# Two early loads issued by ScalarE instead of SyncE, and unit 3's clip and exponential moved up, in a fused gated-attention and gated-MLP kernel

## The chip, the cores and the metric

The kernel runs on one core of one Trainium2 chip. The metric is the time of one execution in microseconds (us), as the device reports it; the time of before is the median of 3 runs. A profile is one execution taken by the hardware profiler. Engine names are those of its rows: PE (TensorE matmuls), PEld (its weight loads), DVE (VectorE), ACT (ScalarE), POOL (GpSimd), SP (SyncE, which only issues transfers here).

## The reference

```python
def _attn_ref(q, k, v, f_logit):           # B=4, H=8, S=768, D=48
    f = 1.0 / (1.0 + np.exp(-f_logit))
    for t in range(S):
        state = f[:, :, t, :, None] * state + np.einsum('bhd,bhe->bhde', k[:, :, t], v[:, :, t])
        y[:, :, t] = np.einsum('bhd,bhde->bhe', q[:, :, t], state)

def _moe_ref(x, w_in, w_spatial, b_spatial, w_out):   # x: (4, 768, 384), d_ff 1024
    h = np.maximum(x @ w_in, 0.0)
    u, v = (h[..., :d_ff // 2], h[..., d_ff // 2:])
    v_n = (v - mean(v)) / np.sqrt(var(v) + 1e-06)
    v_s = np.einsum('ts,bsd->btd', w_spatial, v_n) + b_spatial[None, :, None]
    return (u * v_s) @ w_out
```

The output of the attention, with its heads joined, is the `x` of the second part.

## The kernel before

The recurrence is worked in 24 **units** n = 0 to 23 of 128 time steps (four batches of six). Inside a unit the decay is turned into running sums of logarithms, keys and queries are scaled by exponentials of these sums, and the unit is then two 64-step chunks of ordinary matmuls plus a carried state. The second part (named V, U, S, P and O in the plan) is dense matmul work on what the units leave.

There is no scheduler. `PLAN` is one long list of steps, written by hand or by a search, and the kernel emits the steps in that order. Each engine runs its own instructions in the order of emission, and waits where data or a buffer is missing. A step named `x:n` calls `step_x(n)`; one step issues on one engine, mostly. `BESIDES` lists steps that run on another engine, or in another variant, than their default.

The steps that matter here, by unit n:

- `LF:n` loads the logits (for the first eight units from `fn`, 192 KB) into `ins[n % 3]`; `LK:n` loads keys and queries (512 KB) into the same tile, `LQ:n` the values (192 KB); `LV:i` loads 768 KB of words of `w_in`. The profile names the tiles `fkq`, `val` and `words`. All are issued by SP.
- `c:n` clips the logits (DVE L371, for units in `BESIDES` POOL), `e:n` is an exponential and a logarithm (ACT L375, L376), `z:n` sums along time by a triangular matmul (PE L386), `g:n` and `h:n` are two exponentials of the sums (ACT L397 and L392).
- `k:n` scales the keys (DVE L403; it needs `LK:n` and `g:n`), `q:n` the queries (DVE L407; it needs `LK:n` and `h:n`).
- `X:n` makes the scores (PE L432; it needs `k:n` and `q:n`), `m:n` masks them (DVE L442), `w:n` copies a part of them (ACT L438), `YS:n` multiplies scores by values (PE L484), `kv:n` makes what the unit adds to the state (PE L456), `r0:n`, `r1:n` add this to the state (DVE L462 to L470), `r2:n` decays it, `Yq:n` multiplies queries by the state (PE L496), `ys:n` copies the result out (ACT L500), `xt:n` transposes it (PE L509).
- `ca:V,i` scales the high words of a weight (ACT L307), `ct:V,i` puts low and high words together (three DVE instructions, L312 to L314; the second needs `ca`).
- `D:1,2,512` is two matmuls with no use for the result.

`ins` has three tiles, so unit 3 reuses unit 0's: `LF:3` can be issued only when `k:0`, the last reader of unit 0's logits, is done on DVE.

Of the kernel before, what the change touches and what calls it, by code (L numbers as in the profile page):

```python
# [1004 lines left out]
```

## Time and profile before

| | |
|---|---|
| time, median of 3 | 338.81 us (338.53 to 338.96) |
| time of the profiled execution | 337.91 us |
| its span, first to last instruction | 336.2 us |
| PE busy | 324.4 us, 96% of the span |
| DVE busy | 252.4 us, 75% |
| ACT busy | 182.7 us, 54% |
| POOL busy | 39.7 us, 12% |
| bytes moved by DMA | 38.37 MB |
| granted TensorE clock, mean | 0.999 |

PE is busy for nearly the whole span, so the time is PE's work plus PE's idle time. The idle time lies almost wholly in the first 25 us, and this is where the change stands. The row of shares over the whole span does not show this; the stretches and the waits do.

### The profile page before, as it was taken

The numbers are of one execution on the slowest core, as the hardware profiler recorded it, in microseconds if no ns is written. First come the engines' busy times: TensorE is split into PE (matmuls) and PEld (weight loads), VectorE is DVE, ScalarE is ACT, GpSimd is POOL, SyncE is SP. The second block draws the span as 40 slices with busy tenths as digits, with TensorE's granted clock in tenths as the row PEclk, the third lists the DMA queues.
The fourth block names the chain that finished last, engine by engine and source line by source line (L and its number), as shares of the span: only waits on it lengthen the run. The fifth ranks groups of instructions, "written<-read, shape, count | busy, mean of one in ns | idle before, by whom it ended". The sixth has DMA issues, their size and how long they took to land.

```text
span 336.2 us, 10500 instructions
## 1 busy us (share of the span) xinstructions
PE 324.4 (96%) x4558; PEld 303.5 (90%) x4558; DVE 252.4 (75%) x498; ACT 182.7 (54%) x389; POOL 39.7 (12%) x44
## 2 busy tenths in 40 slices
...
GB/s 230 368 225 280 268 176 225 218 173 47 152 89 237 41 89 155 82 62 126 137 120 142 96 73 202 156 0 24 2 0 0 49 0 25 71 0 26 48 34 118
DMA packets 16581, 38.37 MB, mean 114 GB/s; under 512 B 1552, under 2 KB 11792, under 8 KB 16528
## 3 DMA queue, kind: packets, MB, share of 16 engines
...
q14 instruction: 15, 0.12, 0.1%
HBM read 32.90 MB, written 4.72 MB: 112 GB/s over the span
## 4 chain that ended last, share of the span: by engine, by line
PE 93%; DMA 3%; DVE 1%; ACT 1%; issue 1%; SPq 0%; DVEq 0%; ACTq 0%
PE mm L664 15%; PE mm L547 13%; PE mm L650 13%; PE mm L803 12%; PE mn L739 8%; PE bp L432 5%; PE mm L739 5%; PE bp L496 4%; PE bp L484 3%; PE mn L803 3%; PE mn L650 3%; PE mm L509 2%; PE bp L456 2%; PE mn L547 2%; DMA fkq<-fkq 2%; DMA fkq<-fn 1%
## 5 line engine op out<-in xcount | busy, mean ns | idle before, releaser
L371 POOL TENSOR_SCALAR fkq<-fkq 112x512 f32<-112x512 f32 (+1 forms) x13 | 22.5, 1729 | 140.2 <-DMA fkq<-fkq 121.8
L789 DVE TENSOR_TENSOR gl<-uT,gh 128x384 fp32r<-128x384 f32 x29 | 16.6, 580 | 19.9 <-ACT gh L785 19.6
L785 ACT CAST gh<-uT 128x384 fp32r<-128x384 f32 x29 | 14.4, 511 | 20.0 <-DVE uT L781 9.8
L392 ACT ACTIVATE F<-fkq 112x512 f32<-112x512 f32 x16 | 10.1, 632 | 26.6 <-DVE fkq L381 14.9
L432 PE MATMUL bp<-q,fkq 48*64 48x112 f32 x768 | 23.6, 260 | 0.1
L403 DVE SCALAR_TENSOR_TENSOR fkq<-fkq 112x512 f32<-112x512 f32 x24 | 16.7, 694 | 5.9 <-ACT fkq L397 4.7
L432 PEld LDWEIGHTS bp<-q,fkq 48*64 48x64 f32 x768 | 19.0, 133 | 2.1 <-issue 1.4
L664 PE MATMUL mm<-w_sph,vnh 128*128 128x384 f32 x96 | 20.1, 345 | 0.0
L381 DVE TENSOR_TENSOR_SCAN fkq<-runs,fkq 112x512 f32<-112x512 bf16 x16 | 19.4, 1217 | 0.5 <-ACT fkq L376 0.4
L664 PE MATMUL mm<-w_spl,vnh 128*128 128x384 f32 x96 | 19.5, 338 | 0.0
L664 PE MATMUL mm<-w_sph,vnl 128*128 128x384 f32 x96 | 19.5, 338 | 0.0
L547 PE MATMUL mm<-w_inh,xTh 128*128 128x512 f32 x63 | 19.2, 412 | 0.0
L650 PE MATMUL mm<-xTh,w_inh 128*128 128x384 f32 x78 | 18.7, 348 | 0.0
L442 DVE TENSOR_TENSOR sc<-bp,mask 128x512 f32<-128x512 f32 x24 | 16.4, 684 | 2.5 <-ACT W L438 2.1
L407 DVE TENSOR_TENSOR q<-fkq,F 112x512 f32<-112x512 f32 x24 | 16.7, 694 | 2.1 <-ACT F L392 2.0
L547 PE MATMUL mm<-w_inl,xTh 128*128 128x512 f32 x63 | 18.1, 396 | 0.0
L547 PE MATMUL mm<-w_inh,xTl 128*128 128x512 f32 x63 | 18.0, 394 | 0.0
L650 PE MATMUL mm<-xTl,w_inh 128*128 128x384 f32 x78 | 17.9, 338 | 0.0
L650 PE MATMUL mm<-xTh,w_inl 128*128 128x384 f32 x78 | 17.9, 337 | 0.0
L484 PEld LDWEIGHTS bp<-val,sc 64*64 64x64 f32 x768 | 13.9, 134 | 4.3 <-issue 1.5
L484 PE MATMUL bp<-val,sc 64*64 64x48 f32 x768 | 16.1, 220 | 1.4 <-DVE sc L442 0.9
L664 PEld LDWEIGHTS mm<-w_spl,vnh 128*128 128x128 f32 x96 | 17.1, 188 | 0.0
...
## 6 DMA issues: line engine op xcount, KB each, us to landing
...
val<-vv SPq DMA_DIRECT2D x24, 192.0 KB, 4.5
out<-osb SPq DMA_DIRECT2D x24, 192.0 KB, 2.4
fkq<-fkq SPq DMA_DIRECT2D x8, 512.0 KB, 5.5
...
fkq<-fn SPq DMA_DIRECT2D x8, 192.0 KB, 4.1
...
```

The costliest lines, as they stand in the source:

```text
L371: (nc.gpsimd if beside("c", n) else nc.vector).tensor_scalar(f, f, -LOGIT_MOST, None, op0=ALU.max)
L381: return nc.vector.tensor_tensor_scan(f[0:DP], runs, f[0:DP], 0.0, op0=ALU.mult, op1=ALU.add)
L403: nc.vector.scalar_tensor_tensor(k, f, 1.0 / F_LEAST, k, op0=ALU.min, op1=ALU.mult)
L407: nc.vector.tensor_tensor(q_of(n)[:, :, :, 0:C], *(x.rearrange("p (j c t) -> p j c t", c=T // C, t=C) for x in (parts(n)[2], Fs[n % 2])), ...
L432: nc.tensor.matmul(sc[to, e, cs], k[dr, at:at + C], q_of(n)[dr, j, chunk], start=True, stop=True)
L484: nc.tensor.matmul(y[to, e, cs], s[rows, keys[e]], v[rows, hd], start=j == 0, stop=False, skip_group_check=True)
L547: nc.tensor.matmul(acc, xs[:, c, ut * P:(ut + 1) * P], ws[:, c, G:FF], start=i == 0, stop=i == 3 * KX - 1)
L650: nc.tensor.matmul(acc[:, 0:TH], ws[:, kx, cs], xs[:, kx, :], start=i == 0, stop=i == 3 * KX - 1)
L664: nc.tensor.matmul(acc[:, 0:TH], vns.of((b, ks))[va][:, cs], w_sp_s[wb][:, ks, th * TH:(th + 1) * TH], start=i == 0, stop=i == 3 * KS - 1,)
L739: nc.tensor.matmul(mm.of(user)[:, 0:TH], x, y, start=n == ks == 0 and i not in (3, 6, 7), stop=n == ks == 2, skip_group_check=True,)
L789: nc.vector.tensor_tensor(lo, uTs.of((b, th, c)), hi.bitcast(F32), op=ALU.subtract)
L803: nc.tensor.matmul(acc[:, ms], gs.of((b, th, c))[ga][:, ts], w_out_s[wb][:, c, ms], start=c == cs[0] == 0 and ga == wb == 0, stop=c == cs[ ...
```

## The change

ScalarE (ACT) instead of SyncE (SP) issues `LK:2` and `LF:3`, and three steps change their place in the plan.

```diff
-    LF:0 constants kq:0 LF:2 c:2 kz c:0 e:0 LF:1 c:1 LK:0 e:2 e:1 z:0 g:0 z:2 LK:1 kq:1 k:0 LK:2 h:0 q:0 LQ:0 z:1
-    D:1,2,512 g:1 k:1 LV:1 X:0 LF:3 LQ:1 m:0 h:1 q:1 g:2 k:2 fm:1 LV:0 w:0 YS:0 kv:0 r0:0 X:1 r1:0 c:3 Yq:0 ca:V,1 LF:5
-    fm:0 e:3 LK:3 z:3 LF:4 m:1 ct:V,1 r2:0 h:2 w:1 ys:0 YS:1 kv:1 q:2 xt:0 X:2 r0:1 r1:1 c:5 Yq:1 ca:V,0 g:3 xh:0 xl:0
+    LF:0 constants kq:0 LF:2 c:2 kz c:0 e:0 LK:2 LF:1 c:1 LK:0 e:2 e:1 z:0 g:0 z:2 LK:1 kq:1 k:0 h:0 q:0 LQ:0 z:1 D:1,2,512
+    g:1 k:1 LV:1 X:0 LF:3 LQ:1 m:0 h:1 q:1 g:2 k:2 c:3 fm:1 LV:0 w:0 YS:0 kv:0 r0:0 X:1 r1:0 Yq:0 e:3 ca:V,1 LF:5 fm:0 LK:3
+    z:3 LF:4 m:1 ct:V,1 r2:0 h:2 w:1 ys:0 YS:1 kv:1 q:2 xt:0 X:2 r0:1 r1:1 c:5 Yq:1 ca:V,0 g:3 xh:0 xl:0
...
-    sm:3,0,1 P:3,1,5 sm:3,0,2 U:3,1,3 P:3,1,3
+    sm:3,0,1 P:3,1,5 sm:3,0,2 U:3,1,3 P:3,1,3 LK:2 LF:3
...
     def step_LF(n):
         b, u = divmod(n, NU)
         if n < SUMMED:
-            nc.sync.dma_start(ins[n % 3][:, 0, 0:HD], fn[n])
+            (nc.scalar if beside("LF", n) else nc.sync).dma_start(ins[n % 3][:, 0, 0:HD], fn[n])
...
     def step_LK(n):
         b, u = divmod(n, NU)
-        nc.sync.dma_start(ins[n % 3][:, 1:3], fkq[b, u, :, 1:3])
+        (nc.scalar if beside("LK", n) else nc.sync).dma_start(ins[n % 3][:, 1:3], fkq[b, u, :, 1:3])
```

The new plan is three lines shorter, so line numbers of the changed kernel are three lower: L363 (`LK`) becomes L360, L357 (`LF`) L354, and so on. Tiles: `fkq_111`, `fkq_112`, `fkq_113` are the input tiles of units 0, 1 and 2 (unit 3 uses `fkq_111` again), `val` values, `words` weight words.

First SP, from its first transfer. Before:

```order
L357 DMA fkq_111<-fn 128x384
L357 DMA fkq_113<-fn 128x384
L357 DMA fkq_112<-fn 128x384
L363 DMA fkq_111<-fkq 128x1024
L363 DMA fkq_112<-fkq 128x1024
L363 DMA fkq_113<-fkq 128x1024
L367 DMA val_114<-vv 128x384
L298 DMA words_159<-w_cv 128x2x768
L357 DMA fkq_111<-fn 128x384
L367 DMA val_115<-vv 128x384
L298 DMA words_160<-w_cv 128x2x768
L357 DMA fkq_113<-fn 128x384
```

And of the change:

```order
L354 DMA fkq_111<-fn 128x384
L354 DMA fkq_113<-fn 128x384
L354 DMA fkq_112<-fn 128x384
L360 DMA fkq_111<-fkq 128x1024
L360 DMA fkq_112<-fkq 128x1024
L364 DMA val_114<-vv 128x384
L295 DMA words_159<-w_cv 128x2x768
L364 DMA val_115<-vv 128x384
L295 DMA words_160<-w_cv 128x2x768
L354 DMA fkq_113<-fn 128x384
```

The third transfer of keys and queries (`LK:2`) and the second load of `fkq_111` from `fn` (`LF:3`) are gone from SP, so `LQ:1` and `LV:0`, which stood behind `LF:3` and its wait for `k:0`, stand right behind `LV:1`.

Then ACT, from unit 0's exponential to the weight words. Before:

```order
L376 ACTIVATE fkq_111<-fkq_111 128x384
L375 ACTIVATE fkq_113<-fkq_113 128x384
L376 ACTIVATE fkq_113<-fkq_113 128x384
L375 ACTIVATE fkq_112<-fkq_112 128x384
L376 ACTIVATE fkq_112<-fkq_112 128x384
L397 ACTIVATE fkq_111<-mm_131 112x512
L392 ACTIVATE F_120<-mm_131 112x512
L397 ACTIVATE fkq_112<-mm_133 112x512
L392 ACTIVATE F_121<-mm_133 112x512
L397 ACTIVATE fkq_113<-mm_132 112x512
L438 COPY W_118<-bp_138 128x384
L307 ACTIVATE words_159<-words_159 128x768
```

And of the change (its next three rows are L372, L373 for unit 3's exponential, then L304 on `words_159`):

```order
L373 ACTIVATE fkq_111<-fkq_111 128x384
L360 DMA fkq_113<-fkq 128x1024
L372 ACTIVATE fkq_113<-fkq_113 128x384
L373 ACTIVATE fkq_113<-fkq_113 128x384
L372 ACTIVATE fkq_112<-fkq_112 128x384
L373 ACTIVATE fkq_112<-fkq_112 128x384
L394 ACTIVATE fkq_111<-mm_131 112x512
L389 ACTIVATE F_120<-mm_131 112x512
L394 ACTIVATE fkq_112<-mm_133 112x512
L354 DMA fkq_111<-fn 128x384
L389 ACTIVATE F_121<-mm_133 112x512
L394 ACTIVATE fkq_113<-mm_132 112x512
```

`LK:2` stands behind unit 0's logarithm (`e:0`), and `LF:3` between `g:1` and `h:1`. `e:3`, which stood behind `ca:V,1`, now stands ahead of it.

Last DVE, from unit 0's mask. Before:

```order
L442 TENSOR_TENSOR sc_116<-bp_138,mask 128x512
L407 TENSOR_TENSOR q_123<-fkq_112,F_121 112x8x64
L403 SCALAR_TENSOR_TENSOR fkq_113<-fkq_113 112x512
L462 COPY sB_127<-bp_139 112x192
L470 TENSOR_TENSOR sA_126<-bp_139,sB_127 112x192
L371 TENSOR_SCALAR fkq_111<-fkq_111 128x384
L442 TENSOR_TENSOR sc_117<-bp_138,mask 128x512
```

And of the change:

```order
L439 TENSOR_TENSOR sc_116<-bp_138,mask 128x512
L404 TENSOR_TENSOR q_123<-fkq_112,F_121 112x8x64
L400 SCALAR_TENSOR_TENSOR fkq_113<-fkq_113 112x512
L368 TENSOR_SCALAR fkq_111<-fkq_111 128x384
L459 COPY sB_127<-bp_139 112x192
L467 TENSOR_TENSOR sA_126<-bp_139,sB_127 112x192
L439 TENSOR_TENSOR sc_117<-bp_138,mask 128x512
```

Unit 3's clip `c:3` (L371, now L368) stands ahead of the two state sums `r0:0` and `r1:0` instead of behind them; nothing else changes place on DVE, PE or POOL.

## Rows read from the trace of the kernel before

**Rows 1.** Stretch, length, then busy us of PE, PEld, DVE, ACT, POOL; clock, DMA.

```profile
10.00:15.00 5.00, 3.22 (x142) 2.66 (x132) 4.60 (x9) 2.89 (x6) 0.87 (x3) 1.00 1.03 365
25.00:336.20 311.20, 307.20 (x4085) 288.92 (x4084) 234.06 (x462) 164.47 (x356) 35.32 (x29) 1.00 0.31 101
```

**Rows 2.** PE's waits from 5 to 25 us: releaser, us, times, longest.

```profile
PE mm L386 <- ACT fkq L376: 6.3, 2, 5.0
PE bp L484 <- DVE sc L442: 0.9, 1, 0.9
PE bp L484 <- ACT W L438: 0.5, 1, 0.5
```

**Rows 3.** The chain of waits from 2 to 21 us: start, us, what.

```profile
2.19 5.89 DMA fkq<-fkq
...
8.91 4.73 DMA fkq<-fn
...
14.92 0.53 ACT fkq L376
15.45 0.96 DVE words L313
...
20.55 0.68 PE bp L484 x32
```

**Rows 4.** SP's issues, and single transfers from issue to landing; DMA queue to 14 us.

```profile
2.19 1.38 SPq L363 DMA_DIRECT2D fkq<-fkq  x3
...
q1 hardware_dynamic: 1731, 4.04, 84.2%
...
fkq<-fn SPq DMA_DIRECT2D x1, 192.0 KB, 2.6
...
fkq<-fkq SPq DMA_DIRECT2D x1, 512.0 KB, 6.7
...
fkq<-fkq SPq DMA_DIRECT2D x1, 512.0 KB, 7.5
```

**Rows 5.** DVE in order of time, 8 to 14.9 us, and one later clip.

```profile
8.19 0.69 DVE L403 SCALAR_TENSOR_TENSOR fkq<-fkq 112x512 f32<-112x512 f32 x1 [1.20 <-DMA fkq<-fkq]
...
9.96 0.69 DVE L403 SCALAR_TENSOR_TENSOR fkq<-fkq 112x512 f32<-112x512 f32 x1 [0.47 <-ACT fkq L397]
10.80 0.69 DVE L442 TENSOR_TENSOR sc<-bp,mask 128x512 f32<-128x512 f32 x1 [0.15 <-PE bp L432]
11.41 0.68 DVE L407 TENSOR_TENSOR q<-fkq,F 112x512 f32<-112x512 f32 x1
12.01 0.69 DVE L403 SCALAR_TENSOR_TENSOR fkq<-fkq 112x512 f32<-112x512 f32 x1
12.70 0.36 DVE L462 COPY sB<-bp 112x192 f32<-112x192 f32 x1
13.09 0.36 DVE L470 TENSOR_TENSOR sA<-bp,sB 112x192 f32<-112x192 f32 x1
13.66 0.61 DVE L371 TENSOR_SCALAR fkq<-fkq 128x384 f32<-128x384 f32 x1 [0.21 <-DMA fkq<-fn]
14.19 0.68 DVE L442 TENSOR_TENSOR sc<-bp,mask 128x512 f32<-128x512 f32 x1
...
18.57 0.35 DVE L371 TENSOR_SCALAR fkq<-fkq 128x384 f32<-128x384 f32 x1
18.84 0.55 DVE L525 TENSOR_TENSOR xTl<-mm,xTh 128x384 fp32r<-128x384 f32 x1
```

**Rows 6.** ACT in order of time: unit 0's logarithm, `g:1`, `ca:V,1`.

```profile
4.33 0.52 ACT L376 ACTIVATE fkq<-fkq 128x384 f32<-128x384 f32 x1
...
9.33 0.60 ACT L397 ACTIVATE fkq<-mm 112x512 f32<-112x512 f32 x1 [0.88 <-PE mm L386]
...
13.14 0.91 ACT L307 ACTIVATE words<-words 128x768 f32<-128x768 f32 x1 [1.13 <-DMA words<-w_cv]
```

**Rows 7.** PE: the scores of unit 0 in order of time.

```profile
9.68 1.00 PE L432 MATMUL bp<-q,fkq 48*64 48x112 f32 x32
```

More of the change, by code (lines that the diff above doesn't have):

```diff
@@ new lines @@
+    h:6 q:6 vc:0,2 U:0,0,1 ur:0,0,1 Yq:4 ys:4 LQ:5 YS:5 kv:5 r0:5 LK:7 q:7 vc:0,1 xh:3 xl:3 g:7 k:7 X:6 LW:2,0 Yq:5 ch:U,1
+    w:6 xt:4 xh:4 m:6 cl:U,1 LQ:6 xl:4 ys:5 V:0,3 LF:8 c:8 sq:0,0 sq:0,1 sq:0,2 xt:5 xh:5 X:7 LF:9 na:0,0 r1:5 xl:5 nb:0,0
+    nc:0,0 w:7 e:8 LQ:7 YS:6 kv:6 r0:6 LF:10 m:7 vh:0,1 vl:0,1 r1:6 r2:6 z:8 vh:0,0 wh:2,0 vl:0,0 U:0,0,2 V:0,5 YS:7 Yq:6
+    LW:0,1 c:9 e:9 fm:6 kv:7 U:0,1,3 h:8 q:8 g:8 vr:0,5 U:0,0,3 ys:6 k:8 X:8 r0:7 r1:7 Yq:7 fm:8 z:9 LQ:9 LW:1,0 LB LQ:8
+    LF:11 bs:0,5 r2:7 ur:0,0,2 wh:0,1 fm:7 m:8 wl:2,0 wl:0,1 ur:0,0,3 h:9 q:9 vr:0,3 g:9 k:9 LW:0,0 U:0,1,1 xt:6 vh:0,2
@@ new lines @@
+    V:1,2 S:0,0,1 ur:0,0,0 vr:1,2 z:12 LW:1,1 wh:1,1 wl:1,1 sg:0,0,1 sm:0,0,1 sh:0,0,1 sm:0,0,0 sh:0,0,0 xt:9 xh:9 X:11
+    YS:10 bs:1,2 sm:0,0,3 w:11 kv:10 r0:10 m:11 r1:10 r2:10 na:1,0 sl:0,0,0 h:12 g:12 S:0,1,3 sl:0,0,1 q:12 LF:13 LO:0
+    ca:O,0 k:12 sg:0,1,3 S:0,1,2 Yq:10 ys:10 ur:0,1,1 xl:9 YS:11 kv:11 X:12 r0:11 Yq:11 c:13 nb:1,0 r1:11 e:13 ct:O,0 ch:O,0
+    z:13 h:13 g:13 sg:0,1,2 S:0,1,0 xt:10 fm:13 xh:10 nc:1,0 vn:1,2 vn:1,1 q:13 S:0,1,1 vh:1,1 w:12 LF:15 LQ:12 LF:14
+    sg:0,1,0 xl:10 sh:0,0,3 sl:0,0,3 vn:1,0 c:14 vh:1,2 cl:O,0 m:12 vl:1,2 U:0,1,2 ur:0,1,2 V:1,3 ys:11 xt:11 O:0,0,0
@@ new lines @@
+    sg:1,0,2 YS:16 kv:16 r0:16 r1:16 sm:1,0,1 r2:16 S:1,0,3 S:1,1,0 c:19 c:20 Yq:16 z:18 h:18 fm:18 w:17 q:18 m:17 YS:17
+    kv:17 g:18 k:18 ys:16 X:18 sg:1,0,3 od:0,0,2 LQ:18 sg:1,1,0 LF:21 r0:17 Yq:17 xt:13 xh:14 xl:14 od:0,1,0 e:19 z:19 h:19
+    g:19 U:1,0,3 ur:1,0,3 e:20 V:2,2 vr:2,2 ys:17 w:18 xh:13 U:1,0,2 ur:1,0,2 V:2,0 vr:2,0 sm:1,0,3 m:18 k:19 q:19 X:19
+    LF:22 c:21 r1:17 YS:18 kv:18 LQ:20 LQ:19 z:20 sm:1,0,2 xl:13 m:19 sh:1,0,3 sh:1,0,1 xt:15 xh:15 w:19 bs:2,0 sh:1,0,2
+    sl:1,0,2 xl:15 e:21 r0:18 r1:18 sl:1,0,1 r2:18 xt:17 S:1,1,1 xh:17 xl:17 fm:19 h:20 g:20 k:20 xt:16 xh:16 V:2,1 q:20
@@ new lines @@
+    X:23 m:23 ur:1,1,0 fm:22 flag sm:1,1,0 xt:19 O:1,0,1 sh:1,1,1 sl:1,1,1 w:23 xt:20 xh:19 xl:19 oc:1,0,1 vh:2,0 r2:22
+    LQ:23 YS:23 od:1,0,0 kv:23 r0:23 Yq:22 ys:22 sh:1,1,0 check Yq:23 xl:18 bs:2,4 U:2,0,1 ys:23 mst LY:1 V:2,5 V:2,3
+    sm:1,1,2 sh:1,1,2 LY:2 xh:20 LY:3 ts:1 ts:3 vl:2,0 sl:1,1,0 vl:2,1 vr:2,5 bs:2,5 sl:1,1,2 V:3,0 U:2,0,0 vr:2,3 bs:2,3
+    na:2,1 nb:2,1 nc:2,1 vn:2,3 O:1,1,2 U:2,0,3 U:2,0,2 O:1,1,1 th:1 ur:2,0,1 vn:2,5 vh:2,5 vl:2,2 ts:2 LY:4 ts:4 od:1,0,2
+    vn:2,4 xl:20 V:3,2 th:4 vl:2,5 tl:4 vh:2,4 vl:2,4 tl:1 ur:2,0,3 th:2 vh:2,3 vl:2,3 xs:2,1,1 P:2,0,2 th:3 tl:3 ur:2,0,0
```

108 lines of the change are left out of this document (43 added, 65 removed).

## Prediction

> **What bounds the kernel now.** I read the busy time by stretch first. From 25 us to the end PE is busy 307.2 of 311.2 us; from 10 to 15 us only 3.22 of 5, while DVE is busy 4.60 of 5 and the DMA engines are full (share 1.03) [rows 1]. So what is late at 25 us is late at the end, and the early stretch is ruled by DVE and the loads. PE's own waits between 5 and 25 us have three releasers: ACT L376, 6.3 us in two waits, the longest 5.0 us at the start (so the other is 1.3 us, for unit 3's `e:3`); DVE L442 0.9 us; ACT L438 0.5 us [rows 2]. The chain of waits then says what is late: `LK:0`, issued at 2.19 us, lands 5.89 us later at 8.08; `LF:3`, issued at 8.91, lands 4.73 us later at 13.64; then `e:3`, then DVE's weight words, and at 20.55 PE [rows 3].
>
> One reading of that chain has to be corrected. It puts L313 behind `e:3`, but that instruction needs `ca:V,1`, which ran from 13.14 for 0.91 us and was long done [rows 6]; DVE was simply busy until then. DVE's rows show this: from 8.19 to 14.19 us one instruction follows the other, with waits of 0.47 us (for `g:1`), 0.15 us (for `X:0`) and 0.21 us (for `LF:3`) alone [rows 5]. So PE's 1.3 us behind `e:3` is not all to be had: what follows in PE's queue (`X:2`) needs `q:2`, which stands behind `m:1` and the three weight words on DVE. The change is worth what it does to the start of `m:1`, 14.19 us.
>
> **The change, part by part.**
>
> *Order on DVE.* Before, `r0:0` starts at 12.70, `r1:0` at 13.09, `c:3` at 13.66 behind its load, and `m:1` at 14.19 [rows 5]. A clip that waits for nothing gives DVE free 0.27 us after its start (18.57 to 18.84) [rows 5]. If unit 3's logits are there at 12.70, the three take 0.27 + 0.39 + 0.27, so `m:1` could start at 13.63: **0.56 us earlier** (0.21 us of wait, 0.26 us of a quicker clip, the rest the tail of `r1:0`). `r0:0` needs `kv:0` of PE, which is ready as before. `fm:1` and the rest do not move.
>
> *Order on ACT.* `e:3` costs nothing new, but `ca:V,1` now stands behind it. With `c:3` at 12.70, `e:3` runs from about 13.1, two activations 0.56 us apart, and `ca:V,1` from about 14.15 to 15.05. L313 on DVE comes 1.26 us after `m:1` (15.45 against 14.19 [rows 3, 5]), so at 14.89, and waits for `ca`: **0.16 us back**. Without the cover that ACT idled there (1.13 us before `ca` [rows 6]) the whole 1.1 us of `e:3` would show.
>
> *The issue instructions.* SP's issues of this kind follow each other 0.47 us apart (three in 1.38 us [rows 4]). On ACT, `LK:2` stands behind `e:0`, which ends at 4.85 [rows 6]; what follows is the exponential of unit 2, which waits for POOL anyway, so at most 0.1 to 0.2 us shows, and `z:1` and `g:1` are then no later than the loads they meet below. `LF:3` stands behind `g:1` (9.33 plus 0.60) and in front of `h:1`; `q:1` reads `h:1` at 11.41 [rows 5], half a microsecond of cover. The trace of before has no transfer issued by ACT; I bound the issue between 0 and 0.65 us, and take 0.45 us, all hidden.
>
> *`LF:3` past SP's queue.* It is issued about 1 us later than before (9.9 against 8.91), but it no longer stands behind `LQ:0` and `LV:1` in one queue. A 192 KB load alone lands 2.6 us after its issue [rows 4]; sharing the engines with weight words doubles or triples its half microsecond of data, so 2.6 to 3.7 us: landing 12.5 to 13.6. I take 12.9. If the next term is right, DVE comes to `c:3` later than that, so nothing waits.
>
> *`LK:2` out of SP's queue.* This is the term that decides. Before, all transfers go through one queue, q1, which uses 84% of the 16 engines up to 14 us [rows 4], and land in order: `LK:0` 8.08, `LK:1` 2.66 + 6.7 = 9.36, `LK:2` 3.14 + 7.5 = 10.64. Each 512 KB costs 1.28 us when the queue is full. The order is also the order of need: `k:0` waits 1.20 us for `LK:0`, `k:1` starts at 9.96, and `k:2` only at 12.01 [rows 5]. Issued at 4.85 by ACT, `LK:2`'s data come in about 2.1 us later (2.6 less 0.5 for its 192 KB in the lone load), so from about 6.9, with 1.2 us of `LK:0` and all of `LK:1` still to land. The engines are full, so what it gets, they lose. Bounds: if the older queue goes first, `LK:0` loses 0; if the two share evenly, up to 1.28 us, the whole of one such load. I take **0.9 us**, nearer to even shares, since nothing in the rows says that one queue would wait for another; not all of it, since some engines are through with `LK:0` before. `LK:1` then takes the place of `LK:2`, at about 10.6.
>
> The Trainium skill (DMA: Bandwidth & Descriptors, Queues, rings and completion order) says that each DMA engine takes the queues that have work in turn, a packet at a time; by that rule `LK:0` would lose the full 1.28 us and the kernel 0.9 us. No run shown here has two busy queues, so the trace neither bears it out nor denies it.
>
> **The sum.** `k:0` 0.9 us later, so `X:0` on PE starts at 10.58 instead of 9.68 [rows 7], and `m:0` at 11.70 instead of 10.80 (`k:1`, at 10.7 with `LK:1`, would allow 11.3, so `X:0` is the later). `q:1`, `k:2` follow without a gap, `c:3` takes the place of `r0:0` at 13.60, and `m:1` starts at 14.19 + 0.9 - 0.56 = 14.53. With `ca:V,1` 0.16 us too late, `q:2` and all behind it are 0.9 - 0.56 + 0.16 = **0.5 us later**. The later loads are issued by SP on the same releases and land with 1 to 2 us to spare, so nothing is added or caught up; PE behind 25 us passes the delay on. Profiled execution 337.91 + 0.5 = 338.4 us; the median of 3 is 0.9 us above the profiled one, so 338.81 + 0.5 = **339.3 us**, +0.15%. A measurement of this kernel can tell some 0.2% (0.68 us) from no change.
>
> **The rivals.**
>
> 1. *The second queue costs the first nothing* (the older transfers keep their place, or two queues together stall less). `LK:0` and `LK:1` land as before, and `LF:3` lands before 12.7. Then 0.56 - 0.16 = 0.4 us is gained: 338.4 us. For it: nothing in the rows says that a later queue can take time from an earlier one. Against: the engines are full, at 372 and 365 GB/s in both stretches [rows 1], and the bytes due by 10.6 us are the same.
>
> 2. *`LF:3` is no earlier, and `c:3` now stands in front of the state sums* (the slower end). Its issue waits for `k:0` as before, and `LQ:1` and `LV:0` (960 KB) have moved in front of it on SP. If it lands at 13.64 again with `k:0` on time, `c:3` starts at 13.66, `m:1` at 13.66 + 0.53 + 0.39 + 0.27 = 14.85, and `e:3` and `ca:V,1` end at 16.2, another 0.1 us: 0.8 us lost, 339.6 us. It decides from a landing at 13.0 us on, where gain and loss balance. Against it: 2.6 us for a lone load. With `LK:0` late as in the forecast, DVE reaches `c:3` at 13.6 itself, and this rival adds little.
>
> 3. *`LK:2` comes last.* If the engines serve by age of issue, it lands behind `LQ:0` and `LV:1`, at 13.1 (when `ca:V,1` finds its words [rows 6]). `k:2` then waits from 12.01 to 13.2: 1.2 - 0.56 + 0.16 = 0.8 us lost, 339.6 us.
>
> 4. *Nothing to see.* `LK:0` loses about 0.4 us, `LK:1` allows `m:0` at 11.3, and gain and loss nearly cancel (0.5 - 0.56 + 0.16 = 0.1): 338.9 us. The Trainium skill (DMA: Bandwidth & Descriptors, Issuing engines are not separate DMA queues) says that issuing from several engines saves only the issuer's own time; by it alone nothing else would change, 338.8 us.
>
> **Chances and range.** Forecast 0.45 (its own range 338.9 to 339.8: `LK:0` losing 0.5 to 1.28 us; of it 0.15 for fully even shares, 1.28 - 0.56 + 0.16 = 0.9 us, 339.7), rival 1 0.22, rival 2 0.08, rival 3 0.08, rival 4 0.17. Slower by over 0.2% (above 339.49) holds a good third of the forecast and most of rivals 2 and 3: 0.31. Faster by over 0.2% (below 338.13) would need more than rival 1's 0.4 us, up to the 1 us of DVE's waits: 0.12. Within 0.2%: 0.57. The range of 8 in 10 runs from rival 1's time, a little below, to the full shares with a late `ca`: 338.2 to 339.9 us.
>
> **What would show it.** Right: `k:0` on DVE waits for its load until about 9.0 instead of 8.1, `X:0` starts near 10.6, `LK:1` lands near 10.6 and `LK:2` before it; a second DMA queue in the list; `LF:3` lands about 3 us after its issue, and `c:3` waits for nothing; L313 waits for ACT L304; PE's wait before `z:3` shrinks to almost nothing, and waits before `X:0` and `YS:0` grow. Wrong: `k:0` at 8.2 as before (rival 1 or 3, told apart by whether `k:2` waits), `c:3` waiting for its load (rival 2), or a PE clock below 1.00 in the early stretch, where PE now idles at other moments (it was 1.00 from 10 to 15 us with 1.8 us idle [rows 1]).

## The result: 1.0% slower

| | before | after |
|---|---|---|
| time, median of 4 runs each | 338.67 us (338.53 to 338.96) | 342.66 us (341.86 to 343.78) |
| ratio, with its 95% interval | | 1.0103 [1.0065, 1.0141] |
| profiled execution, and its span | 337.91 us, 336.2 us | 343.78 us, 342.0 us |
| granted clock, mean over the span | 0.999 | 0.985 |
| bytes moved by DMA | 38.37 MB | 38.37 MB |

The forecast was 339.3 us in a range of 338.2 to 339.9; the time lies 2.8 us above its upper end. (The plain quotient of the two medians, 1.0118, lies inside the interval.) I read the trace of after in the order in which the prediction read that of before.

The stretches first (columns as in [rows 1]: length, busy us of PE, PEld, DVE, ACT, POOL; clock, DMA share, GB/s):

```profile
10.00:15.00 5.00, 2.66 (x128) 2.23 (x121) 2.59 (x4) 1.49 (x4) 0.35 (x2) 1.00 1.01 369
15.00:20.00 5.00, 3.02 (x88) 2.73 (x92) 4.23 (x8) 4.11 (x8) 0.51 (x1) 0.84 0.53 175
20.00:25.00 5.00, 5.00 (x103) 3.65 (x98) 3.88 (x9) 2.64 (x6) 0.56 (x1) 0.50 0.34 85
25.00:336.20 311.20, 311.15 (x4203) 292.50 (x4196) 237.64 (x468) 166.66 (x360) 34.98 (x29) 0.99 0.32 102
...
18.50:28.50 10.00, 9.84 (x232) 8.26 (x232) 8.27 (x16) 6.75 (x15) 0.56 (x1) 0.50 0.47 137
```

Two things differ from [rows 1]. From 10 to 15 us DVE, which was busy 4.60 us of 5, is busy only 2.59: it waits, and PE with it. And from 18.5 to 28.5 us the granted clock is 0.50, the lower of the two levels (1.2 instead of 2.4 GHz), while PE is busy 9.84 us of 10. A stretch that looks full to the eye does far less work: in it 232 matmuls touch these 10 us, in before 294 (with PE busy 9.43 us).

PE's waits from 5 to 25 us (as [rows 2]):

```profile
PE mm L383 <- ACT fkq L373: 5.0, 1, 5.0
PE bp L493 <- DVE sA L467: 3.0, 1, 3.0
PE bp L481 <- DVE sc L439: 0.9, 1, 0.9
PE bp L481 <- ACT W L435: 0.4, 1, 0.4
```

The wait for `e:3` is gone (6.3 us in two waits are now 5.0 in one), and a longer one stands elsewhere: 3.0 us ahead of `Yq:0` (L493), for the state sum `r1:0` (L467). DVE's rows say why (as [rows 5]; in brackets the idle time and its releaser):

```profile
7.88 0.69 DVE L400 SCALAR_TENSOR_TENSOR fkq<-fkq 112x512 f32<-112x512 f32 x1 [1.00 <-ACT fkq L394]
...
12.12 0.69 DVE L400 SCALAR_TENSOR_TENSOR fkq<-fkq 112x512 f32<-112x512 f32 x1
15.46 0.36 DVE L368 TENSOR_SCALAR fkq<-fkq 128x384 f32<-128x384 f32 x1 [2.65 <-DMA fkq<-fn]
15.74 0.35 DVE L459 COPY sB<-bp 112x192 f32<-112x192 f32 x1
16.12 0.36 DVE L467 TENSOR_TENSOR sA<-bp,sB 112x192 f32<-112x192 f32 x1
16.40 0.68 DVE L439 TENSOR_TENSOR sc<-bp,mask 128x512 f32<-128x512 f32 x1
...
17.79 0.97 DVE L310 SCALAR_TENSOR_TENSOR words<-words 128x768 int32<-128x768 int32 x1 [0.24 <-ACT words L304]
```

`k:0` (7.88) and `k:2` (12.12) stand within 0.3 us of where they stood in [rows 5], and neither waits for its load. Then `c:3` (L368) waits 2.65 us for unit 3's logits, with both state sums and `m:1` queued behind it: `m:1` starts at 16.40 instead of 14.19. The chain of waits (as [rows 3]: start, us, what) names the same load:

```profile
9.52 5.85 DMA fkq<-fn
...
15.46 0.37 DVE fkq L368
...
15.86 0.53 ACT fkq L372
...
16.93 0.82 ACT words L304
...
18.66 1.10 PE bp L481 x32
```

`LF:3` takes 5.85 us from issue to landing (15.37) where the prediction took 3.0. What stands ahead of it is seen in SP's issues in order of time, from 2 us on, and in the transfers issued up to 14 us (queues with packets, MB and share; then size and median us from issue to landing):

```profile
2.19 0.91 SPq L360 DMA_DIRECT2D fkq<-fkq  x2
3.14 0.43 SPq L364 DMA_DIRECT2D val<-vv  x1
3.61 0.54 SPq L295 DMA_DIRECT2D words<-w_cv  x1
4.19 0.88 SPq L364 DMA_DIRECT2D val<-vv  x1
5.11 0.53 SPq L295 DMA_DIRECT2D words<-w_cv  x1
...
q1 hardware_dynamic: 1543, 3.58, 72.7%
q10 hardware_dynamic: 258, 0.69, 12.4%
...
fkq<-fkq ACTq DMA_DIRECT2D x1, 512.0 KB, 7.3
...
fkq<-fn ACTq DMA_DIRECT2D x1, 192.0 KB, 5.8
```

Before, SP's issues from 8 to 11 us were these:

```profile
8.91 0.34 SPq L357 DMA_DIRECT2D fkq<-fn  x1
9.29 0.44 SPq L367 DMA_DIRECT2D val<-vv  x1
9.77 0.43 SPq L298 DMA_DIRECT2D words<-w_cv  x1
```

`LF:3` waited for `k:0`, and `LQ:1` and `LV:0` stood behind it in the same queue, though they wait for nothing. Now nothing holds SP, and `LQ:1` (192 KB) is issued at 4.19 and `LV:0` (768 KB) at 5.11: 960 KB are under way before ACT issues `LF:3` at 9.52. `LV:0` lands at 15.39 and `LF:3` at 15.37. The second queue, q10, is ACT's.

The packets of the two queues show how they meet. These are the queues' rows (packets, MB, share of the 16 engines) in three stretches: 4.4 to 7.8 us, 8.5 to 10.5 us and 11.2 to 12.8 us.

```profile
q1 hardware_dynamic: 428, 1.24, 97.2%
...
q1 hardware_dynamic: 146, 0.42, 52.0%
q10 hardware_dynamic: 111, 0.41, 50.9%
...
q1 hardware_dynamic: 257, 0.64, 103.5%
```

ACT issues `LK:2` at 4.32, but q10 moves nothing before 7.8; its first packet starts at 7.88, when `LK:0` has landed (7.18). From 8.5 to 10.5 us the two queues share the engines evenly. `LF:3`, issued at 9.52, moves nothing before 12.8 either. So of its 5.85 us some 3.3 pass before its first packet (12.87), and only then does it share with `LV:0`. By [rows 4] a load of this size alone took 2.6 us in all. What holds a second queue's first packet back for so long is not shown by any run.

Last PE, the scores of units 0 and 2 (the same 32 matmuls; [rows 7] has those of before):

```profile
9.79 1.00 PE L429 MATMUL bp<-q,fkq 48*64 48x112 f32 x32
...
21.17 1.77 PE L429 MATMUL bp<-q,fkq 48*64 48x112 f32 x32
```

They take 1.00 us at the one level of the clock and 1.77 at the other.

So the profiled execution's 5.87 us have two parts. PE's idle time between 10 and 25 us rose from 2.85 us (before is busy 3.22, 4.50 and 4.43 us in the three stretches) to 4.32: **about 1.5 us are the wait**. The rest, **about 4.4 us, goes mostly to the stretch at 1.2 GHz**. The whole span bears this out:

```profile
PE 328.4 (96%) x4558; PEld 306.9 (90%) x4558; DVE 252.3 (74%) x498; ACT 182.5 (53%) x389; POOL 39.1 (11%) x44
```

In before PE is busy 324.4 us of 336.2 with as many matmuls. Its busy time is up by 4.0 us, its idle time by 1.8 (11.8 to 13.6). About a third of before's idle time, 4.0 us by [rows 1], lies behind 25 us, so it is not almost all in the early part; but that third hardly changes (4.3 us in after). In the four runs of after the time rises from 341.86 to 343.78 us as the mean clock falls from 0.995 to 0.985; carried on to 0.999 that line gives 341.1 us, 2.4 us above before. So of the median's 4.0 us the wait is 1.5 to 2.4 us and the clock the rest (an estimate from these two readings; it puts all that goes with the mean clock down to the clock).

### The profile page after: what moved, and what is told of

It is laid out like the page before. It is cut to its first block, busy times and chain, and to the rows that moved or that the text cites. A ratio compares the mean times of both kernels' runs of the same rounds, so it can differ in the third digit from the quotient of the medians.

```text
span 342.0 us, 10499 instructions
## 1 busy us (share of the span) xinstructions
PE 328.4 (96%) x4558; PEld 306.9 (90%) x4558; DVE 252.3 (74%) x498; ACT 182.5 (53%) x389; POOL 39.1 (11%) x44
## 2 busy tenths in 40 slices
DMA packets 16581, 38.37 MB, mean 112 GB/s; under 512 B 1552, under 2 KB 11792, under 8 KB 16528
## 4 chain that ended last, share of the span: by engine, by line
PE 92%; ACT 3%; DMA 2%; DVE 1%; issue 0%; ACTq 0%; DVEq 0%
PE mm L661 15%; PE mm L647 12%; PE mm L544 12%; PE mm L800 12%; PE mn L736 8%; PE bp L429 5%; PE mm L736 5%; PE bp L481 4%; PE bp L493 3%; PE mn L800 3%; PE mn L647 3%; PE mm L506 3%; PE bp L453 3%; DMA fkq<-fn 2%; PE mm L383 2%; PE mn L544 2%
## 5 line engine op out<-in xcount | busy, mean ns | idle before, releaser
L368 POOL TENSOR_SCALAR fkq<-fkq 112x512 f32<-112x512 f32 (+1 forms) x13 | 21.9, 1685 | 141.7 <-DVE uT L778 39.7
L786 DVE TENSOR_TENSOR gl<-uT,gh 128x384 fp32r<-128x384 f32 x29 | 15.7, 551 | 19.9 <-ACT gh L782 19.6
L429 PE MATMUL bp<-q,fkq 48*64 48x112 f32 x768 | 25.1, 271 | 0.0
L389 ACT ACTIVATE F<-fkq 112x512 f32<-112x512 f32 x16 | 10.1, 633 | 26.1 <-DVE fkq L378 14.5
L429 PEld LDWEIGHTS bp<-q,fkq 48*64 48x64 f32 x768 | 20.2, 140 | 2.1 <-issue 1.8
L493 PE MATMUL bp<-sB,q 48*64 48x48 f32 x384 | 15.9, 223 | 3.0 <-DVE sA L467 3.0
L481 PEld LDWEIGHTS bp<-val,sc 64*64 64x64 f32 x768 | 14.5, 141 | 4.7 <-issue 1.9
L481 PE MATMUL bp<-val,sc 64*64 64x48 f32 x768 | 16.9, 227 | 1.3 <-DVE sc L439 0.9
```

The source lines that it names most:

```text
L368: (nc.gpsimd if beside("c", n) else nc.vector).tensor_scalar(f, f, -LOGIT_MOST, None, op0=ALU.max)
L429: nc.tensor.matmul(sc[to, e, cs], k[dr, at:at + C], q_of(n)[dr, j, chunk], start=True, stop=True)
L481: nc.tensor.matmul(y[to, e, cs], s[rows, keys[e]], v[rows, hd], start=j == 0, stop=False, skip_group_check=True)
L493: nc.tensor.matmul(y[to, e, cs], q_of(n)[dr, j, at // C, 0:C], state[dr, cs], start=False, stop=True, skip_group_check=True)
```

## The experiments

Theory: the load `LF:3` is the loss. The 960 KB that SP's wait had held back now run ahead of it, and the clip, moved up, makes the state sums wait with it. Rivals: `LK:2` in a second queue takes time from `LK:0` (the forecast's own reason), the new order by itself, ACT's queue itself, and the clock. Before itself spreads between executions (338.07 to 343.05 us among those that enter the ratios of the first set), so each ratio is against runs of before in the same set. Plan tokens are shown with their neighbours; `BESIDES` is the list of steps on another engine.

**One part of the change at a time.** First the changed kernel with `LF:3` back on SP:

```diff
-    sm:3,0,1 P:3,1,5 sm:3,0,2 U:3,1,3 P:3,1,3 LK:2 LF:3
+    sm:3,0,1 P:3,1,5 sm:3,0,2 U:3,1,3 P:3,1,3 LK:2
```

> The changed kernel with LF:3 issued by SP again; LK:2 stays on ACT, c:3 and e:3 stay ahead. Theory L (LF:3 on ACT's queue stands behind the 960 KB of LQ:1 and LV:0, which SP now issues without waiting for k:0; it lands at 15.4 instead of 13.6 us, and what stands behind it waits): LQ:1 and LV:0 are held behind LF:3 again, LF:3 lands near 12.7 to 13.6, DVE waits for it 0 to 0.9 us, the granted clock stays 1.00, 338.3 to 339.2 us. Rival O (the new place of c:3 and e:3 costs by itself): still 1 us or more above before. Rival K (LK:2 on ACT costs, by landing late or by taking time from LK:0 and LK:1): still 1 us or more above before, with k:0, k:1 or k:2 waiting longer.

Measured: 339.33 us, ratio 0.9985 [0.9958, 1.0013]: the whole loss is gone. The load, then `c:3` behind it, and `m:1`:

```profile
fkq<-fn SPq DMA_DIRECT2D x1, 192.0 KB, 4.4
```

```profile
13.23 0.36 DVE L368 TENSOR_SCALAR fkq<-fkq 128x384 f32<-128x384 f32 x1 [0.19 <-DMA fkq<-fn]
...
14.17 0.68 DVE L439 TENSOR_TENSOR sc<-bp,mask 128x512 f32<-128x512 f32 x1
```

It lands at 13.14 us. `m:1` starts at 14.17, as before: the 0.56 us that the prediction saw in the order on DVE are not there, because the load is not there at 12.70.

Only the new order of `c:3` and `e:3`, that is before's plan with these two tokens moved, and both loads on SP:

```diff
-    r0:0 X:1 r1:0 c:3 Yq:0 ca:V,1 LF:5 fm:0 e:3 LK:3
+    k:2 c:3 fm:1 ... r0:0 X:1 r1:0 Yq:0 e:3 ca:V,1 LF:5 fm:0 LK:3
```

> Both loads on SP as before; only c:3 stands ahead of r0:0 and r1:0, and e:3 ahead of ca:V,1. Theory L: LF:3 lands at 13.6 as before, c:3 starts there, the state sums stand behind it, and PE waits about 1 us for r0:0; 0.3 to 0.8 us above before, clock 1.00: 339.0 to 339.5 us. Rival O: the wait of PE that this order makes is enough to bring the clock down to half for a stretch, and the time is 341 us or more.

Measured: 339.77 us, 1.0012 [0.998, 1.0044], nothing that can be told. `LF:3` lands at 14.41 in this profile, and `c:3` waits 1.08 us; PE waits 1.4 us ahead of `Yq:0`, which takes the place of its 1.3 us ahead of `z:3`.

Both loads on ACT, the clip and exponential in the old order:

```diff
-    k:2 c:3 fm:1 ... r0:0 X:1 r1:0 Yq:0 e:3 ca:V,1 LF:5 fm:0 LK:3
+    k:2 fm:1 ... r0:0 X:1 r1:0 c:3 Yq:0 ca:V,1 LF:5 e:3 fm:0 LK:3
```

> Both loads on ACT as in the changed kernel; c:3 and e:3 in their old places. Theory L: LF:3 lands at 15.4, c:3 starts at 15.5 and m:1 at 16.0 instead of 14.2; the state sums and Yq:0 run before the wait, so PE's idle time lies between Yq:0 and z:3 (14.3 to 17.0, 2.7 us) instead of before Yq:0; 1.6 to 2 us above before if the clock stays (340.3 to 340.7), 341 to 343 us if the clock falls to half as in the changed kernel. Rival O (order is the cause): 338.7 us, as before. Rival K (LK:2): the same 341 to 343 us, but with k:2 waiting.

Measured: 341.94 us, 1.0053 [1.0014, 1.0092]. `LF:3` is late here too (15.81), and `c:3` waits 1.27 us, but the state sums are done by then.

Only `LK:2` on ACT, all else as before (`LK:2` behind `e:0`, and alone added to `BESIDES`):

```diff
-    LF:0 constants kq:0 LF:2 c:2 kz c:0 e:0 LF:1 ... k:0 LK:2 h:0
+    LF:0 constants kq:0 LF:2 c:2 kz c:0 e:0 LK:2 LF:1 ... k:0 h:0
```

> Only LK:2 is issued by ACT, behind e:0; LF:3 on SP and the order of c:3 and e:3 as before. Theory L: LK:0 and LK:1 land as early as in the changed kernel (7.2 and 8.5 us) or as before (8.1 and 9.4), LK:2 near 11.6, in time for k:2 at 12.0; LF:3 on SP at 12.7 to 13.6; time within 0.4 us of before, 338.3 to 338.8 us. Rival K (LK:2 on ACT is the cost): 1 us or more above before. What the prediction said (LK:0 loses 0.9 us): 0.5 us above before or more.

Measured: 339.88 us, 0.9983 [0.9957, 1.001]. `LK:2` lands 8.0 us after its issue, at 12.11, and `k:2` does not wait. The term that the forecast called the deciding one costs nothing here.

Only `LF:3` on ACT, in before's plan (`BESIDES` with `LF:3` added, no token moved):

> Only LF:3 is issued by ACT; LK:2 on SP, c:3 and e:3 in their old places. Theory L: LQ:1 and LV:0 stand in front of LF:3, which lands at 15.3 us or later; PE idles 2 to 3 us before z:3; 0.3 to 1% above before, like the run with both loads on ACT in the old order (1.0053). Rival K (LK:2 on ACT made the loss of that run): within 0.2% of before.

Measured: 340.75 us, 1.0041 [1.0011, 1.007]. `LF:3` lands at 15.30, `c:3` waits 1.53 us, and PE's two waits before L383 are 7.3 us where before has 6.3 [rows 2]. By the ratios the load alone makes two fifths of the loss (by its interval, up to two thirds).

The changed kernel with `LK:2` back on SP, the one combination that was left (its place behind `k:0`, `BESIDES` without it):

> The changed kernel with LK:2 back on SP; LF:3 on ACT and the new places of clip and exponential stay. Theory (LF:3 and the order together are the loss, LK:2 takes no part): LF:3 lands at 15.2 to 15.8, c:3 waits 2 to 2.7 us, and the time is 0.8 to 1.2% above before, that of the changed kernel. Rival (LK:2 on ACT's queue ahead of LF:3 holds it up): LF:3 lands at 14.5 or earlier, and the time is 0.4 to 0.6% above before, as with the load alone in the old order.

Measured: 344.08 us, 1.0135 [1.012, 1.0151]. PE's wait, then DVE's:

```profile
PE bp L493 <- DVE sA L467: 3.1, 1, 3.1
```

```profile
16.43 0.36 DVE L368 TENSOR_SCALAR fkq<-fkq 128x384 f32<-128x384 f32 x1 [2.71 <-DMA fkq<-fn]
```

`LF:3` lands at 16.33. The load and the order together are the whole loss, and more than the sum of 0.4% and 0.1%; `LK:2` takes no part in it that can be told. With this the three parts of the change (`LK:2`, `LF:3`, the order) have been run in all eight combinations.

The changed kernel once more, in the set of the kernel with only `LF:3` on ACT and of the next one:

> The changed kernel once more, beside the experiments of this call. Theory L (LF:3 on ACT's queue stands behind LQ:1 and LV:0, which SP no longer holds back; c:3 and all behind it wait, and PE idles about 3 us, after which the clock falls to half in some executions): 0.7 to 1.4% above before, PE waits 2.5 to 3 us before Yq:0. Rival C (chance: the first runs fell on executions with a low clock, as before has them too on a chip whose before spreads from 338 to 345 us): within 0.3% of before.

Measured: 343.51 us, 1.0106 [1.0082, 1.0129]; the same loss. PE waits 3.1 us ahead of `Yq:0`, and the clock is 0.50 from 20 to 25 us again. `LK:2` lands at 13.08 here, and `k:2` waits 0.84 us for it.

**What makes the load late.** The changed kernel with `LV:0` behind `LF:5` in the plan, so that 768 of the 960 KB are held back:

```diff
-    k:2 c:3 fm:1 LV:0 w:0 YS:0 kv:0 r0:0 X:1 r1:0 Yq:0 e:3 ca:V,1 LF:5 fm:0
+    k:2 c:3 fm:1 w:0 YS:0 kv:0 r0:0 X:1 r1:0 Yq:0 e:3 ca:V,1 LF:5 LV:0 fm:0
```

> The changed kernel with LV:0 (768 KB) put behind LF:5 in the plan, so that SP issues it after 12.8 us; LQ:1 alone (192 KB) still stands in front of LF:3. Theory L: LF:3 lands at 12.5 to 13.3 us instead of 15.4, c:3 waits at most 0.6 us, no long wait of PE before Yq:0; time 0.3% below to 0.1% above before. Rival S (ACT's queue is slow by itself, whatever SP's queue holds): LF:3 lands 5 us or more after its issue again, at 14.5 or later, and the time is 0.5% or more above before.

Measured: 341.7 us, 1.006 [1.0036, 1.0084]. `LF:3`, and `c:3` behind it:

```profile
fkq<-fn ACTq DMA_DIRECT2D x1, 192.0 KB, 4.9
```

```profile
14.23 0.36 DVE L368 TENSOR_SCALAR fkq<-fkq 128x384 f32<-128x384 f32 x1 [0.97 <-DMA fkq<-fn]
```

It lands at 14.14, 1.2 us earlier than in after, and the loss falls from 1.06% to 0.60% (the two intervals touch). The theory's own figures were missed (a landing at 12.5 to 13.3, and the time of before): the landing is still a microsecond behind that of `LF:3` from SP in the first experiment, and the time is in the range of the rival S, whose landing (14.5 or later) was missed too. So the 768 KB are a part of the lateness and not the whole; the next runs take ACT's queue out.

All loads on SP, `LF:3` behind `LV:0`. In this kernel the clip of unit 3 came to stand ahead of its load, so it clips what the tile held before, and that part of the computation is changed. Both diffs that follow are against the kernel with the new order alone:

```diff
-    X:0 LF:3 LQ:1 m:0 ... k:2 c:3 fm:1 LV:0 w:0
+    X:0 LQ:1 m:0 ... k:2 c:3 fm:1 LV:0 LF:3 w:0
```

> No load on ACT: all are issued by SP, but LF:3 behind LQ:1 and LV:0 in SP's own queue; c:3 and e:3 in their new places. Theory L (the loss comes from what stands in front of LF:3, not from ACT issuing it): LF:3 lands at 15.4 us or later (up to 16.4, if the single queue is served in order), c:3 waits 2.5 us or more, PE idles 3 us or more before Yq:0, and the time is 1% or more above before, as the changed kernel's. Rival S (ACT's queue is slow by itself): LF:3 lands at 13.6 to 14.5, and the time is within 0.3% of before.

Measured: 343.86 us, 1.0132 [1.0096, 1.0168]. The issue also waited for that clip (14.20), and the load landed at 16.59, so this run does not tell the bytes ahead of it from the late issue. The next has both loads ahead of `LF:3` and the clip behind it:

```diff
-    X:0 LF:3 LQ:1 m:0 ... fm:1 LV:0 w:0
+    X:0 LQ:1 LV:0 LF:3 m:0 ... fm:1 w:0
```

> All loads on SP and LK:2 there as before, the clip and the exponential of unit 3 at their new places, and LQ:1 and LV:0 (960 KB) ahead of LF:3 in SP's queue. Theory (the load is late because the 960 KB stand ahead of it): LF:3 is issued at about 9.3 us and lands at 15.3 to 15.9, right behind LV:0; c:3 waits 2 to 3 us for it, PE waits 2 to 3 us ahead of Yq:0, and the time is 0.7 to 1.2% above before. Rival (the second queue itself makes it late): in SP's queue it lands by 14.4 as in the kernel with the new order alone, and the time is within 0.3% of before.

Measured: 343.83 us, 1.0144 [1.0119, 1.0168]. Loads issued from 5.5 to 9.6 us, then PE's wait, then DVE's:

```profile
words<-w_cv SPq DMA_DIRECT2D x1, 768.0 KB, 10.2
...
fkq<-fn SPq DMA_DIRECT2D x1, 192.0 KB, 7.2
```

```profile
PE bp L493 <- DVE sA L467: 4.0, 1, 4.0
```

```profile
16.72 0.36 DVE L368 TENSOR_SCALAR fkq<-fkq 128x384 f32<-128x384 f32 x1 [3.70 <-DMA fkq<-fn]
```

No transfer is issued by ACT here, and the loss is the changed kernel's or more. `LF:3` lands at 16.63, right behind `LV:0` (16.10). So the 960 KB ahead are enough for the loss, and it needs no second queue: in that, `LF:3` landed together with `LV:0`, in SP's queue behind it.

The changed kernel with `LF:3` issued by ACT ahead of `g:1`:

```diff
-    h:0 q:0 LQ:0 z:1 D:1,2,512 g:1 k:1 LV:1 X:0 LF:3 LQ:1
+    h:0 LF:3 q:0 LQ:0 z:1 D:1,2,512 g:1 k:1 LV:1 X:0 LQ:1
```

> The changed kernel with the issue of LF:3 on ACT moved from behind the exponential g:1 to ahead of it. Theory (bytes ahead decide): issued at about 9.0 instead of 9.5 us, it still lands behind LV:0 at 15.0 to 15.6, and the time stays 0.8 to 1.2% above before. Rival (the late issue on ACT is what costs): it lands 0.5 us or more earlier than in the changed kernel, near 14.5, c:3 waits about 1.5 us instead of 2.65, and the time is 0.5 to 0.7% above before.

Measured: 342.88 us, 1.0103 [1.0088, 1.0118], but the profiled execution alone took 339.47. Its rows: the two loads (`LV:0`, issued at 4.91, then `LF:3`), PE's wait, DVE's, and two stretches:

```profile
words<-w_cv SPq DMA_DIRECT2D x1, 768.0 KB, 10.7
...
fkq<-fn ACTq DMA_DIRECT2D x1, 192.0 KB, 6.0
```

```profile
PE bp L493 <- DVE sA L467: 2.1, 1, 2.1
```

```profile
14.53 0.36 DVE L368 TENSOR_SCALAR fkq<-fkq 128x384 f32<-128x384 f32 x1 [1.21 <-DMA fkq<-fn]
```

```profile
15.00:20.00 5.00, 3.74 (x119) 3.15 (x123) 4.66 (x10) 4.74 (x9) 0.51 (x1) 1.00 0.64 219
20.00:25.00 5.00, 4.43 (x163) 3.56 (x157) 4.93 (x10) 3.71 (x8) 0.56 (x1) 1.00 0.65 185
```

Issued at 8.39, the load lands at 14.44, ahead of `LV:0` (15.6): the rival had the landing right, and in the second queue `LF:3` is slowed by the 960 KB without having to wait for the last of them. The load takes 6.0 us from issue to landing, in after 5.85, so 1.1 us of earlier issue gave 0.9 us of earlier landing: the late issue on ACT (9.52; from SP it was 8.91) is a part of the late landing, about 0.5 of the 1.7 us by these two profiles (an estimate).

But the median is that of after, as the theory had it. The five executions show what goes with this: 339.47 us at a mean clock of 0.997, and 342.71, 342.88, 342.96 and 343.24 at 0.988 to 0.990. The same program with the same order of work is 3.2 to 3.8 us slower at the lower mean clock. The time that these clocks take away (span times one minus the clock) is 1.0 us in the first and 3.4 to 4.1 in the others, so 2.4 to 3.1 us of the difference are the clock (an estimate); the four were not traced.

The traced execution shows what a wait costs where the clock stays, though with a wait of 2.1 us and not 3.0. It is 1.6 us above the traced execution of before (339.47 - 337.91), which is from the first result; in its own set it is only 0.2 us above the median of before (339.23; 338.93 to 339.84). So this wait costs 0.2 to 1.6 us, and the 1.5 us worked out above for the longer one is not contradicted.

**The clock.** In the four profiles in which PE waited 3.0 us or more ahead of `Yq:0` (3.0, 3.1, 3.1, 4.0), the clock fell to 1.2 GHz within 2 us of the end of that wait, in one of them before its end, and stayed there for 3 to 10 us. Of the nine others without fillers in which PE waited 0.9 to 2.3 us ahead of `Yq:0` or `z:3`, it fell in three (the new order alone, both loads alone, and the first order with all loads on SP) and stayed at 1.00 in six. PE's work is the same 4558 matmuls in all of these: where the clock stayed they keep it busy for 324.4 to 325.3 us, where it fell for 325.8 to 328.5. Before itself is not free of it: one of its executions in the first set has a mean clock of 0.982 and takes 343.05 us. Three kernels put matmuls with no use for the result (so their work is added, none is left out) into PE's idle time. The changed kernel with ten ahead of `Yq:0`:

```diff
-    X:1 r1:0 Yq:0 e:3
+    X:1 r1:0 D:3,10,512 Yq:0 e:3
```

> The changed kernel with ten more matmuls that nobody reads (some 2.1 us at full clock) between X:1 and Yq:0 on PE, where it waits 3 us. The load is as late as in the changed kernel (LF:3 at 15.4), m:1 starts 2.2 us later than before, and nothing of the wait is gained back. Theory L with the clock as the second part of the loss: the granted clock stays 1.00 from 15 to 30 us, and the time is 2 to 2.6 us (0.6 to 0.8%) above before, 0.3 to 0.8% below the changed kernel. Rival: the clock has no part, the time is that of the changed kernel or more.

Measured: 342.4 us, 1.0077 [1.0049, 1.0105]; the load landed at 16.27 in this profile and the clock was 0.69 from 20 to 25 us, so it was not held at 1.00 there. The time is nevertheless in the theory's range, with ten matmuls more to do 1.1 us below the changed kernel of the same set (the two intervals overlap). The mean clock of the eight executions is 0.995 to 1.000, that of the changed kernel's six 0.981 to 0.989, and the traced one is one of the two slowest. This speaks for the clock's part, and not against it. With twenty in three places (`D:4,3,512` behind `X:0`, `D:3,15,512` behind `r1:0`, `D:5,2,512` behind `m:1`):

> The changed kernel with 20 matmuls that nobody reads in all three idle stretches of PE between X:0 and YS:1 (three behind X:0, fifteen before Yq:0, two before YS:1). The load is as late as in the changed kernel. If the clock makes a part of the loss: granted clock 1.00 from 15 to 30 us in the profile, and 0.6 to 0.8% above before instead of 1.0 to 1.1. If it has no part: 1.0 to 1.1% above before, or more.

Measured: 349.74 us, 1.0276 [1.0246, 1.0305]. And before with ten (three behind `X:0`, five behind `Yq:0`, two behind `c:5`):

> The kernel before with ten matmuls that nobody reads in its three idle stretches of PE (three behind X:0, five before z:3, two behind c:5 on the way to YS:2). Nothing on the path needs them. If executions of before that take over 339.5 us are ones whose clock fell after such a stretch: the slow ones go, the spread narrows to 338.1 to 339.3 us, and the ratio is 0.995 to 0.999. If the spread has another cause: 0.999 to 1.001, with the same spread.

Measured: 342.61 us, 1.0081 [1.005, 1.0111]. By their times neither of these two bears the clock out: the first falls under the reading that the clock has no part (1.0 to 1.1% above before, or more), the second outside both of its readings. But in their profiles the clock stayed at 1.00 up to 30 us, which fits a fall that follows PE's idle time, though one profile each does not show it, and the fillers cost more than they kept: in the kernel with twenty the stretches from 10 to 20 us hold 4.88 and 5.00 us of PE's work, of which a good part is filler, PE is idle 1.8 us again between 30 and 60 us, and later it waits 4.1 us once (from about 219 us, for nothing that the profile shows), with the clock at 0.57 from 220 to 228 us:

```profile
10.00:15.00 5.00, 4.88 (x139) 3.22 (x138) 2.58 (x4) 1.88 (x4) 0.35 (x2) 1.00 1.00 367
15.00:20.00 5.00, 5.00 (x87) 2.93 (x89) 3.49 (x7) 3.41 (x7) 0.52 (x1) 1.00 0.58 205
```

So these two do not price the clock; the kernel with `LF:3` ahead of `g:1` and the busy time of the same matmuls do it better.

**A way to have the load early.** All loads on SP, the new order, and `LV:1` (768 KB) behind `LF:3`:

```diff
-    g:1 k:1 LV:1 X:0 LF:3 LQ:1
+    g:1 k:1 X:0 LF:3 LV:1 LQ:1
```

> All loads on SP; c:3 and e:3 in their new places; LV:1 (768 KB) behind LF:3 instead of in front of it. Theory L: LF:3, issued at about 8.9, lands at 11.7 to 12.5 us; c:3 waits for nothing, m:1 starts about 0.5 us earlier than before, ca:V,1 finds its words at 13.7 to 14.2; 0.05 to 0.2% below before. Rival O (the new order costs by itself): 0.1% or more above before.

Measured: 341.54 us, 1.0043 [1.0022, 1.0064]. `LF:3` lands at 12.96, 3.9 us after its issue, and `c:3` waits for nothing. `LV:1` now lands at 14.90, but `ca:V,1` stands behind `e:3` until 15.36 anyway; the weight words wait 0.31 us for it, as in the kernel with the new order alone (0.32). The expected gain is not there. The profiled execution took 339.55 us at a clock of 1.00, as much as before in its set (339.6), and the median is 2 us above it. The other nine executions say with what: six have a mean clock of 0.985 to 0.990 and take 340.9 to 342.0 us, two have 0.998 and take 339.97 and 340.19, and one takes 342.06 at 0.997. So the loss goes with the clock in most of them, though PE's wait ahead of `Yq:0` is only 0.3 us in the one that was traced; why it fell in the others was not settled.

No kernel here is measurably faster than before; the nearest, `LK:2` alone on ACT (0.9983) and with the new order (0.9985), both have intervals that hold 1.

## Why the prediction was wrong

- *"`LF:3` past SP's queue"* is the step that failed. It gave the load 3.0 us from issue to landing and put the landing at 12.9 us; the load took 5.85 us and landed at 15.37, and at 15.3 to 16.3 in every profile where ACT issued it behind `LV:0` in SP's queue and behind `g:1`. (The issue was 0.4 us earlier than worked out, 9.52 and not 9.9.) The working took a lone load's 2.6 us [rows 4] and let it share with weight words for half a microsecond of data. It did not ask what SP would do once nothing held it: the wait of `LF:3` for `k:0` had also kept `LQ:1` and `LV:0` back until 9.29 and 9.77 us. With the 960 KB put ahead in SP's own queue the loss came back without any transfer on ACT (1.0144); with `LV:0` held back it shrank to 0.6%. The 960 KB are not all of it: the load took 4.9 us even with `LV:0` held back, and 3.9 on SP with `LV:1` put behind it as well, so the 2.6 to 3.7 us were too few for any of these queues. And some 3.3 of the 5.85 us passed before its first packet, which a lone load does not show.
- *Rival 2* had the mechanism: the 960 KB in front, and `c:3` ahead of the state sums. It was mis-sized and given 0.08. It took the old landing, 13.64, as its case; `c:3` then started at 13.66 and the cost was 0.8 us. In the run `c:3` started at 15.46, and `m:1` was 2.2 us late, not 0.66. The row for the bound would have been the engines' own rate: 960 KB at the 365 GB/s of [rows 1] are 2.7 us (an estimate). Put behind the old landing they give 16.3 us, and after's 15.37 lies between the two.
- *"`LK:2` out of SP's queue"* was wrong. `LK:0` lost nothing: `k:0` starts at 7.88 us after the change, 8.19 before [rows 5], and the move alone is 0.9983. In the nine profiles with `LK:2` on ACT `LK:0` lands at 6.8 to 8.4 us, in the eight with it on SP at 7.2 to 8.9. What gets late is `LK:2` itself: 11.6 to 13.1 us instead of 9.8 to 11.4, at the end where rival 3 had it, and in four of the nine profiles `k:2` waited 0.28 to 0.84 us for it. By the Trainium skill (DMA: Bandwidth & Descriptors, Queues, rings and completion order), queues with work are taken in turn. The trace agrees once both queues move packets (52.0% and 50.9% of the engines from 8.5 to 10.5 us). The prediction had the sharing nearly right and its start wrong: it let the data of `LK:2` come in 2.1 us after the issue, from 6.9 us on, with 1.2 us of `LK:0` and all of `LK:1` still to land. The first packet came 3.6 us after the issue, at 7.88, when `LK:0` had landed. That no loss came of the term is therefore not a sign that a second queue costs nothing.
- *"Order on DVE"*: the 0.56 us needed the load by 12.70. With the load on SP it was there at 13.14 and 14.41, and `m:1` gained nothing (14.17, and 15.44 where the load was there at 14.41). The time worked out for the three instructions, 0.93 us, was right (0.93 to 0.95 in these two and in the kernel with the load in time). With a late load the order turned into a price: the loss is 0.4% in the old order (1.0041) and 1.35% in the new one (1.0135), since DVE holds `r0:0`, `r1:0` and with them `Yq:0` behind the clip; the sum had this price only under rival 2.
- *"Order on ACT"* was right in mechanism: L310 waits 0.24 us for `ca:V,1`, where 0.16 was worked out; 0.32 in the kernel with the load in time.
- *"The issue instructions"* were right in cost: 0.38 and 0.33 us each, and hidden. Their moment was not: the prediction let them start when the activation ahead of them ends (4.85 and about 9.9), and they started within 0.1 us of its start (4.32 beside 4.32, 9.52 beside 9.44).
- *The clock* was no term of the sum, only named among what would make it wrong. It is the larger part of the profiled execution (4.0 to 4.4 of 5.87 us), and some half of the median's 4.0 us. In every profile with an early fall PE had just been idle or still was; what decides it in one execution and not in another of the same kernel was not found.
